# Retention and gated MLP: the first batch's V products in two steps, a new written order, single steps on other engines

## The chip, the core and the metric

The kernel runs on one NeuronCore of a Trainium2 chip. TensorE (PE, with its weight loads PEld) multiplies, VectorE (DVE), ScalarE (ACT) and GpSimd (POOL) do the elementwise work, and loads and stores go out through SP's queue. The metric is device time in microseconds, the median of three runs.

## What is computed

Inputs are q, k, v of shape (4, 8, 768, 64) in float32. A retention layer (a linear attention with a decay for each head) is followed by an MLP with a spatial gate:

```python
for t in range(S):                      # S = 768
    state = gamma * state + outer(k[t], v[t])          # per batch and head
    y[t] = scale * q[t] @ state
x = y as (4, 768, 512)
h = relu(x @ w_in);  u, v = h[..., :512], h[..., 512:]
v_n = (v - mean(v)) / sqrt(var(v) + 1e-6)
v_s = einsum('ts,bsd->btd', w_spatial, v_n) + b_spatial[None, :, None]
return (u * v_s) @ w_out
```

## The kernel before

The retention is cut into 24 groups g: four batches of six blocks of 128 positions. The MLP works on one batch at a time, in two halves of 384 positions. Most matmuls of the MLP are made of three: each operand is split into a high and a low part in a reduced float32 format (F32R), and high x high, high x low and low x high are added in PSUM. That is why every tile has a "high" cast and a "low" subtraction. The weights arrive as 64-bit words and are split on the chip as well.

The order of everything is written by hand: STEPS is one string of 1283 words. A word is a letter and a number; the letter names a step, and the last lines of the kernel call them one by one. Each engine runs its own instructions in the order in which they are written (keep, L151), so a word's place sets what it stands behind on its engine, and semaphores between engines do the rest. The letters that the text uses:

- Loads on SP: G (q and k of a group, from group 9 on the values apart by J), L (a weight slice), K (a slice of w_spatial). B loads the bias.
- Splitting weight slice i: a (absolute value, ACT), c (five DVE steps: c00 is step 0 of slice 0), H (high, ACT), R and Q (the rest and its sum, POOL or DVE by the hundreds digit: R101 is slice 1 on DVE).
- Retention: p scales the values of a group (POOL, by 2xx on ACT), q the scores, j their mask (DVE), t adds to the running total in PSUM (t1xx with the next group's scores), k copies the total to SBUF (ACT, line 371), S and x the same later on as a change that is added, y the outputs, E evicts and scales them (DVE, line 468, four of 128 columns for each group), h and l their high and low parts.
- MLP: V is one k slice (of four) of the V product of a block (V53: block 5, slice 3), r its relu, s, A, e, w, n, N the normalisation. u and z are the U product and its relu. Batch 0 multiplies with w_spatial directly (P; g, i). Batches 1 to 3 use seven products for a panel instead of eight: T sums parts (POOL, line 566), C casts one (ACT, line 582), b is its low half (DVE, line 160), M the product of nine matmuls, F and O the additions and the multiplication (DVE). M105 is product 5 of panel 0 in batch 1. f and d split the gated result, o multiplies it with w_out, Z stores.
- U is a number of matmuls on a zero tile that fill TensorE's time, m prepares the decay (m2 its rows on DVE, m0 a matmul, m1 a copy), v copies constants.

PSUM has the pools ps_r (2 banks), ps_m (3) and ps_o (3). In SBUF the split parts of products and weights live in four buffers of tag "ca" (L193): whoever allocates a fifth waits until one is free. Which buffer a tile gets is worked out when the kernel is built. All matmuls go through mm (L154), all low halves through residue (L160), so their rows are told apart by their tiles.

Of the kernel before, what the change touches and what calls it, by code (L numbers as in the profile page):

```python
# [9 lines left out]
F32 = mybir.dt.float32  # L10
# [6 lines left out]
ALU = mybir.AluOpType  # L17
# [78 lines left out]
def tile_retention_gmlp(  # L96
# [30 lines left out]
    mpool = ctx.enter_context(tc.tile_pool(name="mlp", bufs=2))  # L127
    ps_r = ctx.enter_context(tc.tile_pool(name="ps_r", bufs=2, space=bass.MemoryType.PSUM))
# [33 lines left out]
    def pick(n):  # L162
        return (nc.gpsimd, nc.vector, nc.scalar)[int(n)]

# [68 lines left out]
    def split_high(i):  # L233
        keep(nc.scalar.copy(doubles[i][0], halves[i][1]))
# [35 lines left out]
    def spatial_high(n, s):  # L270
        keep(nc.scalar.copy(parts_sp[n][0][:, s], wholes[n][s]))

    def spatial_low(n, s):
        high, low = parts_sp[n]
        keep(residue(nc.vector, low[:, s], wholes[n][s], high[:, s]))
# [93 lines left out]
    def total_copy(g, i, r):  # L369
        dst = states[g][:, 1] if i == 0 else states[g + 1][:, 0]  # L370
        keep(nc.scalar.copy(dst[ROWS[r]], total[0][ROWS[1 - r]]))
# [126 lines left out]
    def v_products(b, c, ks=range(KT)):  # L498
        xh, xl = xhalf[b, c // TT]
        cols = slice((c % TT) * P, (c % TT) * P + P)  # L500
        if not ks[0]:
            norm[b, c] = ps_m.tile([P, DM], F32, tag="m", name=f"v{b}_{c}")
# [421 lines left out]
```

## Time and profile before

| what | value |
|---|---|
| median of 3 runs | 370.76 us (370.67 to 370.95) |
| the profiled execution | 371.19 us |
| its span, first to last instruction | 369.2 us |
| TensorE busy | 360.7 us, 98% |
| VectorE busy | 240.2 us, 65% |
| ScalarE busy | 156.0 us, 42% |
| POOL busy | 115.0 us, 31% |

Times in the profile are counted from the first instruction. A row of the timeline gives the start, the length, the engine, the line, the operation, out<-in with the tiles' names, and in brackets how long the engine had been idle and what ended that. Rows of one kind in a row are merged (x3). A matmul is drawn longer than the distance to the next one, since matmuls are pipelined, and each one in float32 or F32R on 64 rows is recorded as two. Shares of busy time are averages over stages with different limits, so the table by stage stands beside them.

### The profile page before, as it was taken

To read this page: it belongs to the slowest core of one execution; us is meant where nothing else is said; L and a number is where in the kernel's file an instruction comes from. 1 tells how busy PE (TensorE), PEld (TensorE's weight loads), DVE (VectorE), ACT (ScalarE), POOL (GpSimd) and SP (SyncE) were. 2 spreads that over 40 slices of the span, in tenths; PEclk is the share of its full clock that TensorE was granted. 3 is DMA by queue.
4 is the path that set the end of the run, shared out by engine and by line. 5 is a ranking of instruction groups with operands and counts; after the bars stand their busy time and mean duration, and the time that the engine had idled before them with its cause. 6 is when DMAs were issued, how large, how long until landed. Compare 5 with 4: busy or idle time off the path is not lost.

```text
span 369.2 us, 10325 instructions
## 1 busy us (share of the span) xinstructions
PE 360.7 (98%) x4425; PEld 314.6 (85%) x4428; DVE 240.2 (65%) x533; ACT 156.0 (42%) x322; POOL 115.0 (31%) x121
## 2 busy tenths in 40 slices
PE   7889999999999999999999999999999999999995
PEld 3678885879888889999988889999998888999885
DVE  2999999598866677697685563278575443165631
ACT  4698784443412355632323246242133245432232
POOL 3523621461054224242325341233142321404011
PEclk9999999999999999999999999999999999999999
DMA  8965786012253530303333114113303002000022
GB/s 305 393 236 218 293 298 279 0 33 83 95 167 115 172 142 5 115 3 115 115 117 137 63 59 144 40 76 115 118 0 135 10 2 87 0 0 2 1 87 85
DMA packets 13005, 41.20 MB, mean 112 GB/s; under 512 B 1440, under 2 KB 1696, under 8 KB 12960
## 3 DMA queue, kind: packets, MB, share of 16 engines
q1 hardware_dynamic: 12816, 40.42, 30.0%
q8 instruction: 35, 0.57, 0.6%
q10 hardware_dynamic: 144, 0.13, 0.1%
q14 instruction: 10, 0.08, 0.1%
HBM read 34.25 MB, written 6.29 MB: 110 GB/s over the span
## 4 chain that ended last, share of the span: by engine, by line
PE 95%; DVE 4%; issue 1%; DVEq 0%
PE u L154 18%; PE v L154 18%; PE o L154 18%; PE y L154 10%; PE sp L154 8%; PE x L154 6%; PE z L154 5%; PE s L154 3%; PE d L154 3%; PE w L154 3%; PE wps L734 1%; DVE room L205 1%; DVE xf L468 1%; DVE room L223 0%; DVE room L210 0%
## 5 line engine op out<-in xcount | busy, mean ns | idle before, releaser
L154 PE MATMUL u<-xh,winu_w 128*128 128x384 f32 x256 | 68.3, 338 | 0.0
L154 PE MATMUL v<-winv_w,xh 128*128 128x512 f32 x192 | 60.8, 398 | 0.0
L154 PE MATMUL o<-wout_w,gh 128*128 128x512 f32 (+1 forms) x192 | 59.8, 392 | 0.0
L468 DVE SCALAR_TENSOR_TENSOR xf<-x,decay_t,qd_t 128x128 f32<-128x128 f32 x96 | 29.2, 344 | 29.6 <-PE x L154 23.9
L154 PEld LDWEIGHTS u<-xh,winu_w 128*128 128x128 f32 x256 | 46.5, 188 | 0.7
L154 PE MATMUL u<-xl,winu_w 128*128 128x384 f32 x128 | 42.9, 335 | 0.0
L154 PE MATMUL y<-sp,a 128*128 128x384 f32 x216 | 42.0, 338 | 0.0
L154 PEld LDWEIGHTS v<-winv_w,xh 128*128 128x128 f32 x192 | 35.2, 188 | 7.5
L154 PEld LDWEIGHTS o<-wout_w,gh 128*128 128x128 f32 x192 | 35.2, 188 | 7.0
L566 POOL TENSOR_TENSOR vn<-vn 128x384 f32<-128x384 f32 x24 | 24.8, 1034 | 50.3 <-DVE a L160 41.3
L582 ACT CAST a<-vn 128x384 fp32r<-128x384 f32 x42 | 21.0, 512 | 42.9 <-POOL vn L566 28.0
L154 PEld LDWEIGHTS y<-sp,a 128*128 128x128 f32 x216 | 37.8, 188 | 0.5
L154 PE MATMUL v<-winv_w,xl 128*128 128x512 f32 x96 | 37.5, 391 | 0.0
L154 PE MATMUL o<-wout_w,gl 128*128 128x512 f32 (+1 forms) x96 | 37.3, 389 | 0.0
L160 DVE TENSOR_TENSOR a<-vn,a 128x384 fp32r<-128x384 f32 x42 | 23.6, 576 | 13.0 <-ACT a L582 12.8
L532 POOL TENSOR_TENSOR rs<-rs,mhalf 128x1 f32<-128x1 f32 x24 | 15.0, 628 | 50.3 <-DVE rs L528 47.4
L643 ACT ACTIVATE ur<-u 128x384 f32<-128x384 f32 x32 | 15.2, 487 | 36.0 <-PE u L154 32.4
L345 POOL TENSOR_TENSOR vk<-vk,decay_t 128x512 f32<-128x512 f32 x17 | 18.7, 1103 | 34.3 <-DMA vk<-in_float_dram 34.3
L519 DVE BATCH_NORM_STATS2 bst<-vr 128x6 f32<-128x512 f32 x24 | 16.4, 687 | 18.3 <-ACT vr L512 18.3
L154 PE MATMUL s<-qk 64*64 64x64 f32 x768 | 28.1, 222 | 0.0
L154 PEld LDWEIGHTS s<-qk 64*64 64x64 f32 x768 | 25.3, 137 | 2.7 <-issue 2.3
L421 DVE TENSOR_TENSOR ws<-d,ws 64x256 f32<-64x256 f32 x54 | 22.8, 422 | 6.5 <-PE d L154 5.0
(120 smaller groups left out, 673.4 us busy)
## 6 DMA issues: line engine op xcount, KB each, us to landing
qk<-in_float_dram SPq DMA_DIRECT2D x24, 512.0 KB, 4.6
vk<-in_float_dram SPq DMA_DIRECT2D x20, 512.0 KB, 4.6
raw<-in_int_dram SPq DMA_DIRECT2D x12, 512.0 KB, 6.1
out_dram<-ot SPq DMA_DIRECT2D x23, 256.0 KB, 2.1
wst<-in_float_dram SPq DMA_DIRECT2D x4, 576.0 KB, 7.5
third<-in_float_dram SPq DMA_DIRECT2D x3, 512.0 KB, 10.6
values<-in_float_dram SPq DMA_DIRECT2D x1, 552.0 KB, 4.4
bsp_t<-in_float_dram SPq DMA_DIRECT2D x1, 384.0 KB, 7.3
```

The costliest lines, as they stand in the source:

```text
L154: keep(nc.tensor.matmul(out, lhs, rhs, start=start, stop=stop, skip_group_check=shared))
L160: return eng.tensor_tensor(out, whole, high.bitcast(F32), ALU.subtract)
L205: keep(nc.vector.tensor_scalar(a, a, TOP_MAX, TOP_MIN, ALU.min, ALU.max))
L345: keep(engine.tensor_tensor(values[g], values[g], vd, ALU.mult))
L421: keep(nc.vector.tensor_tensor(dst[ROWS[r]], u, states[g][ROWS[r], i], ALU.add))
L468: nc.vector.scalar_tensor_tensor(xf[:, hp], t[hp % 2][:, hp // 2].rearrange("p i c -> p (i c)"), qg_t[:, c, hp : hp + 1], qd_t[:, hp], ALU ...
L519: keep(nc.vector.bn_stats(st, norm[b, c][0]))
L532: keep(nc.gpsimd.tensor_tensor(rs, rs, mhalf, ALU.pow))
L566: nc.gpsimd.tensor_tensor(*{7: (a11, a11, a21, ALU.subtract), 5: (a21, a21, a22, ALU.add), 6: (a21, a22, a11, ALU.subtract), 3: (a21, a12, ...
L582: keep(nc.scalar.copy(t[:, 0], part_whole(b, p, m)))
L643: keep(nc.scalar.activation(u, pu[:, :HALF], AF.Relu))
L734: keep(nc.tensor.matmul(wps, wz[:, :P], wz, start=True, stop=True))
```

## The change

The V steps of the first batch are cut in two: V10xx multiplies with the high part of the weight slice (two matmuls), V20xx with the low part (one). A block's group c = 0 evicts 256 columns at once, without the factor of the group. Steps that ran on one engine can be sent to another by a digit of the word: casts (H, h, k, X, C, f) and relus (r, z) to DVE, lows (b, Y) to POOL, sums (T) and the decay rows by choice. And all 1299 words of STEPS are written anew.

Counted over the whole string, these steps run on another engine: of C, 21 of 42 go from ACT to DVE; of f, 18 of 32; of h, 9 of 24; of z, 8 of 32; of r, 7 of 24; of X, 6 of 21; of k, 4 of 22; of H, one. Of b, 20 of 42 go from DVE to POOL, of Y 14 of 21, and the d on POOL are 19 instead of 11. Of T, 12 of 24 go from POOL to DVE, and the p are 8 on POOL, 6 on DVE and 10 on ACT instead of 19, 0 and 5. The first words, and the places that the prediction speaks of:

```diff
-    "G0 v p0 U10 q0 j0 L0 L2 a0 m2 t00 m0 k000 k001 t01 y00 U301 y01 c00 c01 c02 c03 a2 c20 c21 "
-    "c22 G1 k011 k010 H0 m1 E00 L1 U201 U101 U501 q1 p1 t10 k100 k101 a1 t11 U401 U701 G2 k111 "
...
-    "r1 p206 j6 S6 Q5 l4 V40 V41 V42 s1 A1 e0 w0 E50 E52 E51 e1 A2 E53 h5 c42 H4 V43 l105 n0 V50 "
-    "V51 V52 V53 e2 w2 c43 R104 n2 c44 Q104 N0 N2 r3 u0 r4 u1 w1 n1 s3 A3 e3 s4 A4 e4 w3 n3 N1 p7 "
...
+    "U10 U301 U201 G0 v L0 p100 U101 m102 q0 j0 t00 k1000 m0 a0 c00 c01 k001 y00 y01 L2 a2 c20 "
+    "c02 t01 c21 G1 q1 c22 j1 L1 m1 E00 E02 H0 G2 k011 G3 L3 p1 k010 c03 G4 U501 U401 U701 c23 "
...
+    "E52 s2 w0 A1 e1 V2041 V1042 n0 h5 R5 a6 j6 l105 a7 c70 A2 B w1 n1 V2042 e2 w2 V1043 V2043 "
+    "V1050 V2050 V1033 V1051 V2051 c43 c44 V1052 N0 N1 Q5 r4 V2052 s4 A4 e4 w4 G7 n2 N2 V1053 "
...
+    "T1105 C1105 p13 x1210 z11 y120 y121 E120 E122 b1105 T1106 C106 Y160 b1107 S13 b1106 x1301 "
+    "x1311 F101 T103 C103 C1102 x1300 b102 u16 z116 M105 F105 G16 M106 C1112 C104 b1103 M103 F106 "
...
+    "E142 G17 E143 h114 T1116 C116 C1117 S15 j16 O104 x1501 M111 d12 o12 F111 x1500 b116 x1510 "
+    "T113 C1113 b1113 x1511 M115 F115 M116 M113 F112 F116 F113 O113 p116 b1117 f111 M117 F117 "
...
+    "C315 M306 b1303 M303 C1304 b1304 F306 Z212 F303 O303 f130 M307 F307 O307 C1302 b302 u37 d30 "
...
+    def copied(out, src, on_vector):
+        return (nc.vector.tensor_copy if on_vector else nc.scalar.copy)(out, src)
...
+        if c == 0:
+            for n in (s // 2 for s in steps if s % 2 == 0):
+                both = t[n].rearrange("p h i c -> p h (i c)")
+                keep(nc.vector.tensor_tensor(xf[:, n::2], both, qd_t[:, n::2], ALU.mult))
+            return
...
+        high, low = winv_h[:, k], winv_l[:, k]
+        three = ((xh, high), (xh, low), (xl, high))
+        for x, w in (three, three[::2], three[1:2])[part]:
+            n = begun[b, c] = begun.get((b, c), 0) + 1
+            mm(norm[b, c], x[:, k, cols], w, start=n == 1, stop=n == 3 * KT)
...
-    def part_high(b, p, m):
+    def part_high(b, p, m, on_vector):
         t = pieces[p, m] = pair_room(F32R, f"a{b}_{p}_{m}")
-        keep(nc.scalar.copy(t[:, 0], part_whole(b, p, m)))
-
-    def part_low(b, p, m):
+        keep(copied(t[:, 0], part_whole(b, p, m), on_vector))
+
+    def part_low(b, p, m, engine):
         t = pieces[p, m]
-        keep(residue(nc.vector, t[:, 1], part_whole(b, p, m), t[:, 0]))
+        keep(residue(engine, t[:, 1], part_whole(b, p, m), t[:, 0]))
...
+        "k": lambda n: total_copy(n // 100 % 10, n // 10 % 10, n % 10, n // 1000),
...
+        "V": lambda n: v_products(*divmod(n % 1000 // 10, NC), n % 10, n // 1000),
...
+        "T": lambda n: part_sum(n // 100 % 10, n // 10 % 10, n % 10, pick(n // 1000)),
+        "C": lambda n: part_high(n // 100 % 10, n // 10 % 10, n % 10, n // 1000),
+        "b": lambda n: part_low(n // 100 % 10, n // 10 % 10, n % 10, pick(1 - n // 1000)),
```

## Rows read from the trace of the kernel before

**Rows 1.** The page: busy time by engine, and the chain that ended last.

```profile
PE 360.7 (98%) x4425; PEld 314.6 (85%) x4428; DVE 240.2 (65%) x533; ACT 156.0 (42%) x322; POOL 115.0 (31%) x121
...
PE 95%; DVE 4%; issue 1%; DVEq 0%
```

**Rows 2.** Busy time by stage: stretch, length, each engine, granted clock, DMA share.

```profile
0.00:10.00 10.00, 7.58 (x68) 3.62 (x70) 2.85 (x6) 3.83 (x7) 2.81 (x15) 1.00 0.83 315
10.00:28.00 18.00, 15.74 (x527) 12.58 (x526) 17.67 (x38) 15.43 (x46) 7.53 (x5) 1.00 0.81 310
28.00:60.00 32.00, 32.00 (x388) 25.16 (x385) 30.52 (x73) 24.50 (x55) 13.08 (x14) 1.00 0.78 291
60.00:360.00 300.00, 299.97 (x3426) 268.63 (x3425) 188.15 (x417) 110.28 (x212) 90.63 (x88) 1.00 0.21 75
360.00:369.20 9.20, 5.41 (x33) 4.58 (x31) 0.98 (x2) 1.96 (x4) 0.91 (x1) 0.96 0.24 86
```

**Rows 3.** TensorE's waits, whole span: total us, times, longest.

```profile
PE spread L154 <- DVE sown L821: 1.2, 1, 1.2
PE x L154 <- DVE third L391: 1.0, 1, 1.0
```

**Rows 4.** Timeline of the start: fills, first scores, first scaling, first mask.

```profile
1.25 4.45 PE L734 MATMUL wps<-wz 128*128 128x512 bf16 x10 [1.25 <-DVE wz L794]
5.62 1.43 PE L154 MATMUL s<-qk 64*64 64x64 f32 x26
...
5.72 1.04 POOL L345 TENSOR_TENSOR values<-values 128x512 f32<-128x512 f32 x1 [3.09 <-DMA values<-in_float_dram]
...
7.36 0.69 DVE L391 TENSOR_TENSOR ws<-s,mask_t 128x512 f32<-128x512 f32 x1 [6.17 <-PE s L154]
```

**Rows 5.** Timeline: S6 to the next V, step l105 and what follows, V50, first U.

```profile
41.45 0.23 PE L154 MATMUL s<-qk 64*64 64x64 f32 x2
...
42.49 0.50 PE L154 MATMUL v<-winv_w,xh 128*128 128x512 f32 x1
...
43.60 0.69 DVE L160 TENSOR_TENSOR xl<-xf,xh 128x512 fp32r<-128x512 f32 x1
44.21 0.21 DVE L537 TENSOR_SCALAR nb<-mv,rs 128x1 f32<-128x1 f32 x1
...
45.34 0.39 PE L154 MATMUL v<-winv_w,xh 128*128 128x512 f32 x1
...
48.06 0.33 PE L154 MATMUL u<-xh,winu_w 128*128 128x384 f32 x1
```

**Rows 6.** Groups by line and shape: busy us, mean ns, idle before and its enders.

```profile
L371 ACT COPY ws<-total 64x256 f32<-64x256 f32 x14 | 5.1, 366 | 2.8 <-PE total L154 2.7
L421 DVE TENSOR_TENSOR ws<-d,ws 64x256 f32<-64x256 f32 x54 | 22.8, 422 | 6.5 <-PE d L154 5.0
L160 DVE TENSOR_TENSOR a<-vn,a 128x384 fp32r<-128x384 f32 x42 | 23.6, 576 | 13.0 <-ACT a L582 12.8
L611 DVE TENSOR_TENSOR t<-y,bsp_t 128x384 f32<-128x384 f32 x18 | 10.0, 556 | 6.2 <-PE y L154 5.8
L566 POOL TENSOR_TENSOR vn<-vn 128x384 f32<-128x384 f32 x24 | 24.8, 1034 | 50.3 <-DVE a L160 41.3 <-ACT vn L544 8.8
L582 ACT CAST a<-vn 128x384 fp32r<-128x384 f32 x42 | 21.0, 512 | 42.9 <-POOL vn L566 28.0 <-PE y L154 7.2 <-PE z L154 6.0
```

**Rows 7.** Timeline: one DVE operation beside a POOL instruction, and alone.

```profile
16.15 1.58 POOL L242 TENSOR_TENSOR winv_w<-df,room 128x512 fp32r<-128x512 f32 x1 [2.14 <-DVE room L231]
16.53 1.49 DVE L205 TENSOR_SCALAR room<-room 128x512 f32<-128x512 f32 x1
...
20.54 0.42 DVE L205 TENSOR_SCALAR room<-room 128x512 f32<-128x512 f32 x1
```

**Rows 8.** The products of batch 1: pieces of the chain, and a cast.

```profile
158.06 1.58 PE y L154 x9
...
159.67 0.51 ACT L582 CAST a<-vn 128x384 fp32r<-128x384 f32 x1 [0.23 <-PE y L154]
```

More of the change, by code (lines that the diff above doesn't have):

```diff
@@ L127, in tile_retention_gmlp @@
     mpool = ctx.enter_context(tc.tile_pool(name="mlp", bufs=2))
+    spool = ctx.enter_context(tc.tile_pool(name="small", bufs=3))
     ps_r = ctx.enter_context(tc.tile_pool(name="ps_r", bufs=2, space=bass.MemoryType.PSUM))
@@ L163, in pick, with positive @@
         return (nc.gpsimd, nc.vector, nc.scalar)[int(n)]
+    def copied(out, src, on_vector):
+        return (nc.vector.tensor_copy if on_vector else nc.scalar.copy)(out, src)
+    def positive(out, src, on_vector):
+        if on_vector:
+            return nc.vector.tensor_scalar(out, src, 0.0, None, ALU.max)
+        return nc.scalar.activation(out, src, AF.Relu)
     doubles = [
@@ L231, in split_low, with split_high @@
         keep(nc.vector.scalar_tensor_tensor(a, low, 2.0**-52, a, ALU.mult, ALU.mult))
-    def split_high(i):
-        keep(nc.scalar.copy(doubles[i][0], halves[i][1]))
+    def split_high(i, on_vector):
+        keep(copied(doubles[i][0], halves[i][1], on_vector))
     def split_rest(i, engine):
@@ L268, in spatial_sum, with spatial_high, spatial_low @@
         parts_sp[n] = [slot(SPLIT[n][i], F32R, f"sp{n}_{i}") for i in range(2)]
-    def spatial_high(n, s):
-        keep(nc.scalar.copy(parts_sp[n][0][:, s], wholes[n][s]))
-    def spatial_low(n, s):
+    def spatial_high(n, s, on_vector):
+        keep(copied(parts_sp[n][0][:, s], wholes[n][s], on_vector))
+    def spatial_low(n, s, engine):
         high, low = parts_sp[n]
-        keep(residue(nc.vector, low[:, s], wholes[n][s], high[:, s]))
+        keep(residue(engine, low[:, s], wholes[n][s], high[:, s]))
     queries = {}
@@ L367, in total_sum, with total_copy @@
                 )
-    def total_copy(g, i, r):
+    def total_copy(g, i, r, on_vector):
         dst = states[g][:, 1] if i == 0 else states[g + 1][:, 0]
-        keep(nc.scalar.copy(dst[ROWS[r]], total[0][ROWS[1 - r]]))
+        keep(copied(dst[ROWS[r]], total[0][ROWS[1 - r]], on_vector))
     def score(g, i, hp, r):
@@ L476, in out_evict, with out_half @@
             )
-    def out_half(g, low, engine=None):
+    def out_half(g, low, engine=None, on_vector=False):
         b, c = divmod(g, NC)
@@ L484, in out_half @@
         else:
-            keep(nc.scalar.copy(xh[:, :, cols], outs[g]))
+            keep(copied(xh[:, :, cols], outs[g], on_vector))
     def split3(pairs, ps, start=True, stop=True):
@@ L496, in tile_retention_gmlp, with v_products, v_relu @@
     norm = {}
-    def v_products(b, c, ks=range(KT)):
+    begun = {}
+    def v_products(b, c, k, part=0):
         xh, xl = xhalf[b, c // TT]
         cols = slice((c % TT) * P, (c % TT) * P + P)
-        if not ks[0]:
+        if (b, c) not in begun:
             norm[b, c] = ps_m.tile([P, DM], F32, tag="m", name=f"v{b}_{c}")
-        split3(
-            [((xh[:, k, cols], xl[:, k, cols]), (winv_h[:, k], winv_l[:, k])) for k in ks],
-            norm[b, c],
-            start=not ks[0],
-            stop=ks[-1] == KT - 1,
-        )
-    def v_relu(b, c):
+        high, low = winv_h[:, k], winv_l[:, k]
[3 more added lines that the diff above has]
+            mm(norm[b, c], x[:, k, cols], w, start=n == 1, stop=n == 3 * KT)
+    def v_relu(b, c, on_vector):
         v = mpool.tile([P, DM], F32, tag="v", bufs=3, name=f"vr{b}_{c}")
-        keep(nc.scalar.activation(v, norm[b, c], AF.Relu))
+        keep(positive(v, norm[b, c], on_vector))
         norm[b, c] = [v]
     def v_stats(b, c):
-        st = mpool.tile([P, 6], F32, tag="bst", bufs=2, name=f"bst{b}_{c}")
-        mv = mpool.tile([P, 2], F32, tag="mv", bufs=3, name=f"mv{b}_{c}")
-        rs = mpool.tile([P, 1], F32, tag="rs", bufs=3, name=f"rs{b}_{c}")
+        st = spool.tile([P, 6], F32, tag="bst", bufs=2, name=f"bst{b}_{c}")
+        mv = spool.tile([P, 2], F32, tag="mv", name=f"mv{b}_{c}")
+        rs = spool.tile([P, 1], F32, tag="rs", name=f"rs{b}_{c}")
         keep(nc.vector.bn_stats(st, norm[b, c][0]))
@@ L535, in v_bias @@
         v, mv, rs, _ = norm[b, c]
-        nb = mpool.tile([P, 1], F32, tag="nb", bufs=3, name=f"nb{b}_{c}")
+        nb = spool.tile([P, 1], F32, tag="nb", name=f"nb{b}_{c}")
         keep(nc.vector.tensor_scalar(nb, mv[:, 0:1], rs, -1.0, ALU.mult, ALU.mult))
@@ L561, in corners, with part_sum @@
         return [vn[b][:, s, d] for d in cols for s in rows]
-    def part_sum(b, p, m):
+    def part_sum(b, p, m, engine):
         a11, a12, a21, a22 = corners(b, p)
         keep(
-            nc.gpsimd.tensor_tensor(
+            engine.tensor_tensor(
                 *{
@@ L638, in mlp_u, with u_relu @@
         us[b, half, j] = pu
-    def u_relu(b, j, half):
+    def u_relu(b, j, half, on_vector):
         pu = us[b, half, j]
         u = mpool.tile([P, HALF], F32, tag="u", name=f"ur{b}_{j}_{half}", bufs=6)
-        keep(nc.scalar.activation(u, pu[:, :HALF], AF.Relu))
+        keep(positive(u, pu[:, :HALF], on_vector))
         us[b, half, j] = u
@@ L667, in gate_product @@
     def gate_product(b, j, half):
-        pp, u = gate[b, half, j], us[b, half, j]
+        pp = gate[b, half, j]
         t = mpool.tile([P, HALF], F32, tag="t", name=f"t{b}_{j}_{half}", bufs=3)
@@ L671, in gate_product, with gate_high @@
         keep(nc.vector.tensor_tensor(t, pp[:, :HALF], bsp_t[:, cols], ALU.add))
-        gate[b, half, j] = t, u
+        gate[b, half, j] = t
     def gate_times(b, j, half):
-        t, u = gate[b, half, j]
+        t, u = gate[b, half, j], us[b, half, j]
         keep(nc.vector.tensor_tensor(t, t, u, ALU.mult))
         gate[b, half, j] = t
-    def gate_high(b, j, half):
+    def gate_high(b, j, half, on_vector):
         t = gate[b, half, j]
         gh = mpool.tile([P, HALF], F32R, tag="gh", name=f"gh{b}_{j}_{half}")
-        keep(nc.scalar.copy(gh, t))
+        keep(copied(gh, t, on_vector))
         gate[b, half, j] = (t, gh)
@@ L738, in tile_retention_gmlp @@
     steps = {
-        "m": lambda n: (decay_spread, decay_copy, decay_rows)[n](),
+        "m": lambda n: (
+            decay_rows(pick(n // 100)) if n % 100 == 2 else (decay_spread, decay_copy)[n]()
+        ),
         "v": lambda n: consts_copy(),
@@ L747, in tile_retention_gmlp @@
         "c": lambda n: splits[n % 10](n // 10),
-        "H": split_high,
+        "H": lambda n: split_high(n % 100, n // 100),
         "R": lambda n: split_rest(n % 100, pick(n // 100)),
@@ L754, in tile_retention_gmlp @@
         "t": lambda n: total_sum(n // 10 % 10, n % 10, n >= 100),
-        "k": lambda n: total_copy(n // 100, n // 10 % 10, n % 10),
+        "k": lambda n: total_copy(n // 100 % 10, n // 10 % 10, n % 10, n // 1000),
         "U": lambda n: warm(n % 100),
@@ L760, in tile_retention_gmlp @@
         "E": lambda n: out_evict(n // 10, [n % 10]),
-        "h": lambda n: out_half(n, False),
+        "h": lambda n: out_half(n % 100, False, None, n // 100),
         "l": lambda n: out_half(n % 100, True, pick(n // 100)),
-        "V": lambda n: v_products(*divmod(n // 10, NC), [n % 10]),
-        "r": lambda n: v_relu(*divmod(n, NC)),
+        "V": lambda n: v_products(*divmod(n % 1000 // 10, NC), n % 10, n // 1000),
+        "r": lambda n: v_relu(*divmod(n % 100, NC), n // 100),
         "s": lambda n: v_stats(*divmod(n, NC)),
@@ L773, in tile_retention_gmlp @@
         "W": spatial_sum,
-        "X": lambda n: spatial_high(n // 10, n % 10),
-        "Y": lambda n: spatial_low(n // 10, n % 10),
+        "X": lambda n: spatial_high(n // 10 % 10, n % 10, n // 100),
+        "Y": lambda n: spatial_low(n // 10 % 10, n % 10, pick(1 - n // 100)),
         "u": lambda n: mlp_u(n // 10, *units[n % 10]),
-        "z": lambda n: u_relu(n // 10, *units[n % 10]),
+        "z": lambda n: u_relu(n // 10 % 10, *units[n % 10], n // 100),
         "P": lambda n: spatial_products(0, *units[n]),
@@ L780, in tile_retention_gmlp @@
         "i": lambda n: gate_times(0, *units[n]),
-        "T": lambda n: part_sum(n // 100, n // 10 % 10, n % 10),
-        "C": lambda n: part_high(n // 100, n // 10 % 10, n % 10),
-        "b": lambda n: part_low(n // 100, n // 10 % 10, n % 10),
+        "T": lambda n: part_sum(n // 100 % 10, n // 10 % 10, n % 10, pick(n // 1000)),
+        "C": lambda n: part_high(n // 100 % 10, n // 10 % 10, n % 10, n // 1000),
+        "b": lambda n: part_low(n // 100 % 10, n // 10 % 10, n % 10, pick(1 - n // 1000)),
         "M": lambda n: product(n // 100, n // 10 % 10, n % 10),
@@ L786, in tile_retention_gmlp @@
         "O": lambda n: product_times(n // 100, n // 10 % 10, n % 10),
-        "f": lambda n: gate_high(n // 10, *units[n % 10]),
+        "f": lambda n: gate_high(n // 10 % 10, *units[n % 10], n // 100),
         "d": lambda n: gate_low(n // 10 % 10, *units[n % 10], pick(n // 100)),
@@ L814, in tile_retention_gmlp, with decay_rows @@
         )
-    def decay_rows():
+    def decay_rows(engine):
         n = NP * P // C
@@ L820, in decay_rows @@
         rows = rows_t.rearrange("p (c n) -> p c n", n=n)
-        keep(nc.vector.tensor_tensor(rows, eye, own, ALU.mult))
+        keep(engine.tensor_tensor(rows, eye, own, ALU.mult))
     def decay_spread():
```

111 rows, old and new, of the table STEPS are left out of this document.

## Prediction, made before the change was run

> **What bounds the kernel now.** I read the page's busy line and chain first, then a table of engine time by stage, then what TensorE waited for. The page says TensorE: it is busy for 98% of the span, and the chain that ended last is 95% TensorE [rows 1]. The table by stage says where the other 2% are. From 60 to 360 us TensorE is busy for 299.97 of 300 us; from 28 to 60 us for 32.00 of 32; before 28 us it lacks 2.4 + 2.3 us; the end lacks 3.8 us, which is the last copy and store [rows 2]. "Busy" hides gaps shorter than a matmul's drawn length, so I also compared the starts: twelve matmuls of the last V block run from 45.34 to 48.06 us, 0.227 us each, back to back, and nine matmuls of a product take 1.58 us, a wait-free pace [rows 5, 8]. So after 28 us there is nothing to win short of fewer matmuls. The waits before that are few; the longest are 1.2 us for the decay rows and 1.0 for a mask [rows 3].
>
> Who makes TensorE wait there is read from the same table: from 10 to 28 us VectorE is busy for 17.67 of 18 us and ScalarE for 15.43; from 28 to 60 us VectorE for 30.52 of 32 [rows 2]. In the first 45 us VectorE is as much a bound as TensorE, and after 60 us it is not (188 of 300 us).
>
> **The change, part by part.** The written order of TensorE's work holds the same matmuls: each of the 24 V steps of the first batch keeps its three, as two and one. The 18 fill matmuls stay 18. So TensorE's own work changes by nothing, and the forecast is a sum of waits: in the start, where VectorE decides, and later, where new waits can come.
>
> *The start.* I follow VectorE to one step, l105, the low half of block 5, without which TensorE can't begin that block's V products. Before, l105 starts at 43.60, the next instruction follows at 44.21, and V50 starts at 45.34, about 1.05 us after l105 ends: TensorE comes last [rows 5]. VectorE ran the 74 instructions ahead of l105, and l105 itself, from 7.36 (first mask) to 44.21, 36.9 us [rows 4, 5]. Adding them up at their spacing in a full queue gives 32.4; 4.5 us are collisions and waits. The new order puts 79 ahead instead: four copies of the running total (0.42 each by the nearest VectorE row of that size, 0.37 on ScalarE, [rows 6]: 1.7), the first scaling (0.6), one more sum Q102 (0.6), the cast h103 (0.4), against two evictions of 256 columns for four of 128 (-0.2) and a few small ones (-0.1): 3.0 us more, 35.4 in all.
>
> Two of these, the scaling and the decay rows (1.2 us), now run while VectorE stood idle, from about 5.72, when the first values are there [rows 4]. But three fill matmuls move ahead of the first scores. Ten took 4.45 us, 0.43 each, and the first scores came at 5.62 [rows 4]; three more end at 6.8 if they keep that pace. The granted clock is full in that stretch [rows 2], yet 0.43 is what 512 columns take at 1.2 GHz, while V's 512 columns take 0.227 later, near 2.4 GHz [rows 5]: the engine was at the lower level. Part of the delay comes back, because the scores then run at the faster pace. I take the first mask at 7.95 (bounds 7.4, no delay, and 8.7, all of 1.3). From there 34.2 us of queue remain ahead of the end of l105. If nothing collided or waited, it would end at 42.2; with all of the old 4.5 us at 46.7. I take 2.4: eight long POOL instructions instead of eleven stand ahead of it, and POOL causes most of the 4.5. So 44.6, against 44.2 before.
>
> What is worth the same differs, though. At V50 TensorE had done S6 (about 1.04 us, from 41.45 to 42.49) and 2.7 us of V were left [rows 5]; in the new order S6 comes later and ten V steps, 3.4 us, are left. The moment of equal progress is 45.34 - 1.04 - 0.7 = 43.6. With V1050 at 44.7 the start **loses 1.1 us**. Bounds: a gain of 1.4 (l105 at 42.2) and a loss of 3.2 (46.7). ScalarE points the same way: the scalings p202, p203 and p204 stay on it, each behind copies that wait for TensorE, and t20, t130 and t140 wait for them.
>
> *Casts on VectorE behind buffers.* Twenty-one casts of product parts (C) move from ScalarE to VectorE. The parts live in four buffers of tag ca, so a cast can have to wait until a product ends. The trace shows it on ScalarE: its casts idled 7.2 and 6.0 us for products y and z, for example the one at 159.67, as the product of 158.06 ends [rows 6, 8]. There nothing urgent is queued behind it. On VectorE the additions F are, and a product that accumulates into the same bank waits for its F. Three places in the new order have this form. (1) C1102 stands ahead of x1300, b102, z116 and F105; if its buffer is that of M105, VectorE needs 0.35 + 0.42 + 0.58 + 0.56 + 0.56 = 2.5 us after M105 [rows 6], while only M106 (1.58) covers it before M103: 0.9 us. (2) C1117 waits for M111, then j16, O104, x1501, F111, x1500, b116, POOL's T113 (1.03), C1113 and POOL's b1113 (1.04) must run before M113: about 6.0 us, against 5.2 of cover by o12, M115 and M116: 0.8. (3) C1304 stands ahead of F306 and may wait for M303; M307 is next: 0.35 + 0.56 = 0.9. A cast of 384 columns is not in the trace on VectorE; 0.35 is scaled from its 0.42 for 512, and 0.55, a two-input one, is the other bound [rows 6, 7]. Which cast gets which buffer is fixed when the kernel is built, and I can't read it from the order: each of the three is worth nothing if another cast gets the freed buffer. Together 0 to 2.6; I take **1.3 us lost**.
>
> *Lows on POOL, sums on VectorE.* 34 low halves (20 b, 14 Y) go to POOL, where an instruction of that size takes 1.03 instead of 0.58, and 12 sums T come back [rows 6]. I followed the queues around all products: apart from the three places the lows have over 0.4 us to spare, so I cost them at nothing; the cover is the product before. If it is gone, each costs about 0.5. Here a row speaks against the change: VectorE's clamp takes 0.42 alone, and 1.49 when POOL's sum started 0.38 us ahead of it [rows 7]. The Trainium skill (SBUF — State Buffer, SBUF: two separate sides) says that the two engines share a port pair that one of them holds for its whole instruction while the other blocks, and names VectorE's copies in the two-port mode and its operations on two SBUF inputs; the trace agrees. By that rule alone every meeting of a POOL low with a VectorE cast would cost up to 1.1 us; the sum leaves this to the third rival, priced by the rows.
>
> *Nothing else.* The gate's late read of u, the new pool of small tiles and the first block's evictions without a factor change no queue that ends last. Loads move on SP's queue (L3 now behind a wait for the first qk buffer, L5 and K earlier); their users come over 4 us later. The end (o37, copies, stores) is as before.
>
> **The sum.** Against the profiled execution, 371.19 us with a span of 369.2: 371.19 + 1.1 + 1.3 = 373.6. The median of the runs is 370.76, 0.43 less, so I forecast 373.2 us.
>
> **The rivals.** (a) *The start wins.* VectorE idles until 7.36 now and loses 4.5 us to collisions and waits (one of them is in [rows 7]); if both go, l105 ends at 42.2, 1.4 us are won and no cast waits: 371.19 - 1.4 - 0.43 = 369.4. For it: POOL has less ahead of l105. Against it: 3.0 us more on an engine that is already full. It decides once l105 ends before 43.5. Chance 0.28. (b) *The start draws and the buffers fall kindly*, or the change doesn't do what it says since VectorE sets the start either way: 370.8. Chance 0.14. (c) *Collisions in the product chains.* If six of the 20 products whose low half is now on POOL each wait 0.6 us for it behind a VectorE instruction, 3.6 us come on top of the start's 1.1: 375.5. For it: 1.49 against 0.42. Against it: after 60 us both engines have idle time. Chance 0.10. The forecast itself, 371.3 to 374.9: 0.48.
>
> **How the numbers follow.** 0.2% is 0.74 us, about what a measurement of this kernel can tell from no change. Faster: (a), 0.28. Same: (b), 0.14. Slower: the forecast and (c), 0.58. The range goes from 369.4, the end of (a), to 376.5: the start's loss of 3.2 and the casts' 2.6 on the median, 376.6, rounded.
>
> **What would show it.** First mask near 8.0 us. l105's end, the last V product of batch 0 near 48 us, and TensorE's progress there 1 us behind. TensorE waits of 0.5 to 1 us for VectorE F or POOL low halves between 145 and 190 us and near 320 us, where there are none now. The forecast is wrong if l105 ends before 43.5, or if TensorE shows no waits after 60 us and the time is below 370.0.

## The result and the profile after

The changed kernel takes 376.18 us (375.92 to 376.43), against 370.78 for the kernel before: 1.0145 of it (95% interval 1.0127 to 1.0163), 5.4 us slower. I had forecast slower, by 2.4 us. The profiled execution has a span of 374.6 us, 5.4 over the 369.2 of before.

The page first: busy time by engine, and the chain that ended last.

```profile
PE 362.2 (97%) x4428; PEld 315.0 (84%) x4428; DVE 261.8 (70%) x579; ACT 129.5 (35%) x288; POOL 129.2 (34%) x136
...
PE 87%; DVE 5%; DMA 3%; ACT 2%; issue 1%; SPq 1%; POOL 0%; DVEq 0%
```

TensorE's share of the chain fell from 95% to 87% [rows 1]: there are now places where something else comes last. The table by stage (columns as in [rows 2]; the last two rows are shorter stretches) says where.

```profile
0.00:10.00 10.00, 8.56 (x131) 4.62 (x133) 4.11 (x9) 3.97 (x7) 1.77 (x14) 1.00 0.82 315
10.00:28.00 18.00, 16.00 (x434) 13.10 (x432) 14.89 (x35) 13.37 (x38) 5.12 (x4) 0.91 0.91 344
28.00:60.00 32.00, 31.56 (x414) 25.86 (x414) 30.67 (x78) 23.89 (x57) 13.23 (x14) 1.00 0.77 292
60.00:360.00 300.00, 295.23 (x3396) 261.94 (x3395) 207.16 (x453) 85.25 (x182) 106.02 (x102) 1.00 0.20 70
...
15.00:18.00 3.00, 3.00 (x80) 3.00 (x80) 1.31 (x3) 0.56 (x2) 1.39 (x1) 0.50 0.92 367
145.00:200.00 55.00, 52.49 (x735) 49.01 (x734) 43.20 (x93) 12.18 (x28) 24.08 (x24) 1.00 0.25 88
```

From 60 to 360 us TensorE now lacks 4.8 us, where it lacked 0.03 [rows 2]. Up to 10 us it does more than before; from 10 to 28 us it is busy for as long, but at a lower granted clock. TensorE's waits by what ended them (total us, times, longest):

```profile
PE z L159 <- DVE t L630: 2.5, 2, 1.4
PE s L159 <- DMA qk<-in_float_dram: 1.5, 2, 1.3
...
PE y L159 <- DVE t L630: 1.2, 1, 1.2
PE x L159 <- issue: 1.1, 1, 1.1
```

Three waits for an addition F (line 630), 3.7 us together; one for a load in the start; and one, "issue", for nothing that the profile shows.

A lag worked out from the matmul starts puts them in time. I price each matmul still to come at the mean spacing of its kind in the kernel before after 70 us, look up when that kernel had the same work left, and take the difference. It is good to some 0.3 us. (Rows: kernels of the experiments below; columns: us in the kernel's own time.)

```
                      45   145   165   192   260   270   330   340
changed              0.9   0.7   2.4   3.3   2.7   4.1   4.1   5.5
e2_casts_later       1.3   1.8   1.9   1.2   0.8   2.6   2.7   2.5
e5_start_load       -0.1   0.0   1.5   2.2   2.0   4.3   4.3   5.7
e7_lows_vector       1.5   2.3   4.8   7.1  11.4  11.3  13.8  14.5
e10_load_only        1.1   1.1   1.0   0.5   0.1   0.8   0.8   0.6
```

So the changed kernel loses 0.9 us in the start, 1.7 between 145 and 165 us, 0.9 up to 192, 1.4 at 265 and 1.4 at 332. It wins back 0.2 before 145 us and 0.6 between 192 and 260, for which I have no row.

**The three waits for F.** VectorE, TensorE and GpSimd at the first place, C1102:

```profile
158.74 1.73 PE L159 MATMUL y<-sp,a 128*128 128x384 f32 x9
158.94 0.55 DVE L171 CAST a<-vn 128x384 fp32r<-128x384 f32 x1 [1.61 <-PE z L159]
159.27 1.01 POOL L165 TENSOR_TENSOR a<-vn,a 128x384 fp32r<-128x384 f32 x1 [0.63 <-ACT a L171]
159.52 0.43 DVE L434 TENSOR_TENSOR ws<-d,ws 64x256 f32<-64x256 f32 x1
159.87 0.82 DVE L165 TENSOR_TENSOR a<-vn,a 128x384 fp32r<-128x384 f32 x1
160.71 0.56 DVE L175 TENSOR_SCALAR ur<-u 128x384 f32<-128x384 f32 x1
161.18 0.55 DVE L630 TENSOR_TENSOR t<-z,bsp_t 128x384 f32<-128x384 f32 x1
161.88 0.41 PE L159 MATMUL z<-sp,a 128*128 128x384 f32 x1 [1.41 <-DVE t L630]
```

The cast idles 1.61 us until the product z (M105) has let go of its buffer. Behind it stand x1300, the low b102 (0.82), z116 and only then F105; M103 starts at 161.88, when F105 has ended. M106 (158.74, nine matmuls of 0.17) would have let it start at 160.3: 1.6 us lost. At the third place, C1304, the same happens with F306; at the second the chain from b116 over T113 and C1113 ends with F115 at 188.5, and M113 starts:

```profile
182.29 0.55 DVE L171 CAST a<-vn 128x384 fp32r<-128x384 f32 x1 [0.67 <-PE y L159]
...
185.91 1.01 POOL L585 TENSOR_TENSOR vn<-vn 128x384 f32<-128x384 f32 x1 [8.53 <-DVE a L165]
186.96 0.55 DVE L171 CAST a<-vn 128x384 fp32r<-128x384 f32 x1 [0.78 <-POOL vn L585]
187.59 1.97 POOL L165 TENSOR_TENSOR a<-vn,a 128x384 fp32r<-128x384 f32 x2 [0.67 <-DVE a L171]
188.59 1.66 PE L159 MATMUL z<-sp,a 128*128 128x384 f32 x8 [1.10 <-DVE t L630]
...
332.92 0.55 DVE L171 CAST a<-vn 128x384 fp32r<-128x384 f32 x1 [3.62 <-PE z L159]
333.39 0.55 DVE L630 TENSOR_TENSOR t<-y,bsp_t 128x384 f32<-128x384 f32 x1
334.00 1.33 PE L159 MATMUL y<-sp,a 128*128 128x384 f32 x6 [1.18 <-DVE t L630]
```

Start to start, TensorE loses 1.58, 1.26 and 1.34 us at the three places: 4.2.

**The load in the start.** The first scores come at 5.83 and the first mask at 7.03, ahead of [rows 4]; but q2 then stands ahead of its load, which is issued when it was before (4.14 us), and the granted clock falls to 0.50 from 15 to 18 us (above). That fall is not what makes the kernel slower: it is in the profiled execution, whose mean granted clock is 0.994, and the other three, at 0.998 to 1.000, take 375.92 to 376.42 us.

```profile
13.31 0.33 PE L159 MATMUL x<-qk,ws 64*64 64x64 f32 x6
14.90 0.37 PE L159 MATMUL s<-qk 64*64 64x64 f32 x2 [1.26 <-DMA qk<-in_float_dram]
...
43.78 0.68 DVE L165 TENSOR_TENSOR xl<-xf,xh 128x512 fp32r<-128x512 f32 x1
```

The last row is l105: 43.78, where it was 43.60 [rows 5]. The early scores come from the fills, whose starts stand 0.43 us apart up to 4.7 us and 0.22 after it. The record of the granted clock begins only at that moment (4.66 us), so the 1.00 in the row of the first ten microseconds, here and in [rows 2], does not say at which level the first fills ran. In the profiles of the experiments this record begins anywhere from 4.1 to 7.2 us, and where it begins at 6.9 or later all 13 fills stand 0.43 apart.

**The stop at 265.** Six matmuls of a group of eight, a stop, and the last two:

```profile
264.80 0.30 PE L159 MATMUL x<-qk,ws 64*64 64x64 f32 x6
266.18 0.32 PE L159 MATMUL x<-qk,ws 64*64 64x64 f32 x2 [1.08 <-issue]
```

### The profile page after: what moved, and what is told of

Read it like the earlier page. It is cut to its first block, busy times and chain, and to the rows that moved or that the text cites. A ratio compares the mean times of both kernels' runs of the same rounds, so it can differ in the third digit from the quotient of the medians.

```text
span 374.6 us, 10326 instructions
## 1 busy us (share of the span) xinstructions
PE 362.2 (97%) x4428; PEld 315.0 (84%) x4428; DVE 261.8 (70%) x579; ACT 129.5 (35%) x288; POOL 129.2 (34%) x136
## 4 chain that ended last, share of the span: by engine, by line
PE 87%; DVE 5%; DMA 3%; ACT 2%; issue 1%; SPq 1%; POOL 0%; DVEq 0%
PE u L159 18%; PE o L159 17%; PE v L159 16%; PE y L159 9%; PE sp L159 8%; PE x L159 5%; PE z L159 5%; PE s L159 4%; DMA qk<-in_float_dram 3%; PE w L159 3%; PE d L159 1%; SPq L162 1%; DVE a L171 1%; DVE t L630 1%; DVE xf L486 1%
## 5 line engine op out<-in xcount | busy, mean ns | idle before, releaser
L159 PE MATMUL u<-xh,winu_w 128*128 128x384 f32 x256 | 70.0, 340 | 0.0
L165 POOL TENSOR_TENSOR a<-vn,a 128x384 fp32r<-128x384 f32 x20 | 22.1, 1110 | 50.2 <-DVE a L171 27.4
L486 DVE SCALAR_TENSOR_TENSOR xf<-x,decay_t,qd_t 128x128 f32<-128x128 f32 x80 | 24.3, 345 | 11.5 <-PE x L159 8.0
L159 PE MATMUL s<-qk 64*64 64x64 f32 x768 | 29.7, 224 | 1.5 <-DMA qk<-in_float_dram 1.5
L563 ACT ACTIVATE vn<-vr,nb,rs 128x512 f32<-128x512 f32 x24 | 19.2, 815 | 28.5 <-DVE nb L556 25.0
L165 POOL TENSOR_TENSOR xl<-xf,xh 128x512 fp32r<-128x512 f32 x13 | 17.9, 1379 | 30.3 <-ACT xh L171 14.8
L551 POOL TENSOR_TENSOR rs<-rs,mhalf 128x1 f32<-128x1 f32 x24 | 13.9, 587 | 41.1 <-DVE rs L547 40.5
L165 POOL TENSOR_TENSOR gl<-ur,gh 128x384 fp32r<-128x384 f32 x16 | 16.8, 1052 | 28.2 <-DVE gh L171 13.4
L171 ACT CAST a<-vn 128x384 fp32r<-128x384 f32 x21 | 10.8, 516 | 42.4 <-PE z L159 15.0
L159 PEld LDWEIGHTS u<-xl,winu_w 128*128 128x128 f32 x128 | 24.0, 188 | 0.7
```

The costliest lines, as they stand in the source:

```text
L159: keep(nc.tensor.matmul(out, lhs, rhs, start=start, stop=stop, skip_group_check=shared))
L165: return eng.tensor_tensor(out, whole, high.bitcast(F32), ALU.subtract)
L171: return (nc.vector.tensor_copy if on_vector else nc.scalar.copy)(out, src)
L486: nc.vector.scalar_tensor_tensor(xf[:, hp], t[hp % 2][:, hp // 2].rearrange("p i c -> p (i c)"), qg_t[:, c, hp : hp + 1], qd_t[:, hp], ALU ...
L551: keep(nc.gpsimd.tensor_tensor(rs, rs, mhalf, ALU.pow))
L563: keep(nc.scalar.activation(vn[b][:, c], v, AF.Identity, bias=nb, scale=rs))
```

## The experiments

Moves in the written order are given as the words that change place. The times are medians, with the lowest and highest in brackets; each ratio is against the kernel before on the same chip.

**Casts to ScalarE.**

```diff
-C1102 ... C1117 ... C1304
+C102 ... C117 ... C304
```

> The changed kernel with three of its 21 moved casts put back on ScalarE at the same written places: C1102, C1117 and C1304. Theory (a cast that waits for its buffer on VectorE holds the addition F that TensorE's next product needs): the TensorE waits of 1.58 us at 160, 1.26 at 187 and 1.34 at 332 go, 376.2 - 4.2 = 372.0 us; the 1.3 us stop at 265 stays. Rival (VectorE and GpSimd are simply too full in the product chains, the casts only happen to stand there): the waits come back at other products, 375 us or more.

Measured 375.10 us (374.88 to 375.57), 1.0114 [1.0098, 1.0129]: neither theory's number. The third wait is gone, the second is 0.33, the first is as long as it was. The trace of the first place:

```profile
158.79 0.93 ACT L171 CAST a<-vn 128x384 fp32r<-128x384 f32 x2 [2.21 <-POOL vn L585]
158.86 1.73 PE L159 MATMUL y<-sp,a 128*128 128x384 f32 x9
159.39 1.02 POOL L165 TENSOR_TENSOR a<-vn,a 128x384 fp32r<-128x384 f32 x1 [0.62 <-ACT a L171]
159.76 1.06 DVE L165 TENSOR_TENSOR a<-vn,a 128x384 fp32r<-128x384 f32 x1 [1.85 <-ACT a L171]
161.31 0.55 DVE L630 TENSOR_TENSOR t<-z,bsp_t 128x384 f32<-128x384 f32 x1
162.00 0.41 PE L159 MATMUL z<-sp,a 128*128 128x384 f32 x1 [1.41 <-DVE t L630]
```

The cast now waits on ScalarE, but its low b102 is one of those left on VectorE, ahead of F105, and waits for the cast: 1.85 us idle, then 1.06 beside GpSimd's low. What counts is not which engine waits for the buffer, but that anything that depends on it stands ahead of F on VectorE.

**Casts behind the additions.**

```diff
-C1102 x1300 b102 u16 z116 M105 F105
+x1300 u16 z116 M105 F105 C1102 b102
-C1117 ... M115 F115
+M115 F115 C1117
-C1304 b1304 F306
+F306 C1304 b1304
```

> The changed kernel with the same three casts left on VectorE, but written behind the addition that they held: C1102 and its low b102 behind F105, C1117 behind F115, C1304 and its low b1304 behind F306. If the place in VectorE's queue is the cause, all three waits go, 372.0 us as with the casts on ScalarE. If it is the engine (0.55 us for a cast there, beside GpSimd's lows), 375 us or more.

Measured 373.48 us (372.53 to 374.05), 1.0066 [1.0045, 1.0086]. All three waits for F are gone, with the casts still on VectorE, and the lag doesn't rise from 145 to 260 us. TensorE's longest waits, one for a zero tile in the start left out:

```profile
PE x L159 <- issue: 1.7, 2, 1.3
...
PE x L159 <- DVE xf L482: 0.8, 1, 0.8
```

And at the first place, the timeline: F105 (160.01) runs as soon as M105 has ended, and M103 (161.38) follows M106 without a gap.

```profile
158.26 1.72 PE L159 MATMUL z<-sp,a 128*128 128x384 f32 x9
159.82 1.72 PE L159 MATMUL y<-sp,a 128*128 128x384 f32 x9
160.01 0.56 DVE L630 TENSOR_TENSOR t<-z,bsp_t 128x384 f32<-128x384 f32 x1 [0.57 <-PE z L159]
161.38 1.03 PE L159 MATMUL z<-sp,a 128*128 128x384 f32 x5
```

The place in the queue is shown as the cause. The median gains 2.7 us rather than 4.2. In its profile the start was 1.1 us later (lag at 145: 1.8 against 0.7): its 13 fills took 5.51 us, and 4.65 in the changed kernel. That would be most of the difference, if the other executions, of which there is no trace, started as late; this is not shown. Over all profiles with the three fills ahead the 13 take from 4.37 to 5.73 us, and the first scores begin from 5.5 to 6.9 us.

**The output products apart.**

```diff
-S21 ... y200 y201 M215
+S21 ... M215 y200 y201
```

> The changed kernel with the output products y200 and y201 moved behind the product M215, so that they no longer follow the step S21 directly. Theory (TensorE stopped for 1.3 us at 265 because the unbroken run of short 64-row matmuls of S21, y200 and y201 uses up its instructions faster than they come): the stop goes, 376.2 - 1.3 = 374.9 us. Rival (it belongs to a spot in the instruction stream or to the output and load transfers begun at that moment): a stop of the same size stays close by, 376.2 us.

Measured 377.02 us (375.43 to 377.50), 1.0149 [1.0120, 1.0179]: no gain. The stop inside y201 is gone, as the theory said, but M211 follows y201 now and waits 0.8 us for an output eviction (1.0 start to start):

```profile
PE y L159 <- DVE xf L486: 0.8, 1, 0.8
```

**V in one step again.**

```diff
-V1000 ... V2000
+V00
```

(and so for all 24, each at the place of its second part)

> The changed kernel with the first batch's V products in one step again, each standing where its second part (the low half of the weights) stood. TensorE is full from 28 us on, so what the split brings can only be idle time before that: V1000 filled 0.45 us at 18.5, and one or two more first parts stand ahead of their second. Theory: the split is worth about 0.5 to 1 us, 376.7 to 377.2 us. Rival (VectorE up to l105 sets the start whatever TensorE does before): 376.2 us.

Measured 377.53 us (376.76 to 378.38), 1.0178 [1.0156, 1.0200], 0.3% over the changed kernel's ratio, as the theory has it, though the two intervals overlap. The lag at 32 us is 1.9, against 0.8, and stays at 2.0. But this profile's fills took 5.73 us, 1.1 more than the changed kernel's, and a kernel with V split and fills as slow (the one with o22 moved, below) has a lag of 2.2 at 60 us too. So the split helps early, by some 1 us at 32, and what is left of it at the end of the start is between nothing and 1.2 us: not settled.

**The load G2 first.**

```diff
-L1 m1 E00 E02 H0 G2
+G2 L1 m1 E00 E02 H0
-a1 c10 Q0 L5 k100 k101 j2
+Q0 L5 k100 k101 a1 j2 c10
```

> The changed kernel with one change in its start: the load G2 is issued ahead of L1, and the weight clamp's two first steps a1 and c10, which use L1, stand behind k101 and j2. In the changed kernel TensorE waited 1.45 us at 13.4 us for this load and then ran at a granted clock of 0.50 from 15 to 18 us. Theory (that wait costs the start its whole loss): the wait goes and the start wins about 1 to 1.5 us, 374.7 to 375.2 us. Rival (VectorE up to l105 sets the end of the start, the wait lies beside it): TensorE idles somewhere else before 45 us and the time stays 376.2 us.

Measured 376.62 us (375.87 to 377.79), 1.0147 [1.0118, 1.0175]: the time is the rival's. Its profile isn't: the lag is about 0 from 45 to 145 us. The rows of l105 (a timeline) and of the stretch from 10 to 28 us (the table by stage):

```profile
42.98 0.68 DVE L165 TENSOR_TENSOR xl<-xf,xh 128x512 fp32r<-128x512 f32 x1
```

```profile
10.00:28.00 18.00, 14.89 (x455) 12.12 (x449) 16.22 (x37) 14.41 (x42) 5.52 (x4) 1.00 0.95 353
```

l105 starts 0.8 us earlier than in the changed kernel, with the same instructions ahead of it, and VectorE is busy for 16.22 us instead of 14.89: it followed the load, not its own length. In the same profile the 0.7 us are lost again at 262: S21 waits 0.6 us start to start, for G22's load by the next experiments. Whether all its executions did, the single profile can't say. The rival is right in part, too: TensorE now stops inside q2's scores, for 0.8 us at 14.1, and for 0.5 at 19.6, both "issue" (last section).

**Casts mended, o22 behind S21.**

```diff
-o22 l18 x2000 ... S21
+l18 x2000 ... S21 o22
```

> The changed kernel with the three casts behind their additions (372.5 to 374.1 us alone) and, for the stop at 265, the output product o22 moved behind the step S21, so that 12 long matmuls stand between the short ones of S21 and those of y200 and y201. Theory (the stop comes when short matmuls run on without a break until an instruction block has to be fetched): the stop of 1.3 to 1.5 us goes, 372.1 us. Rival (the stop moves to the next wait, as when the y steps stood behind M215): 373.5 us.

Measured 375.08 us (372.78 to 376.33), 1.0085 [1.0047, 1.0123]. The stop inside y201 is gone again, and again something takes its place: S21, 2.7 us earlier in TensorE's order, waits for its load.

```profile
261.75 0.33 PE L159 MATMUL s<-qk 64*64 64x64 f32 x4 [1.29 <-DMA qk<-in_float_dram]
```

Its executions fall in two groups. Two, at a mean granted clock of 1.000, take 372.8 us, near the 372.1 of the theory; three, at 0.949 (the profiled one) to 0.995, take 375.1 to 376.3. No trace shows the first two.

**Lows back to VectorE, sums back to GpSimd** (on the kernel with the casts mended).

```diff
-b1101 ... b1317 (20 words)   T1105 ... T1316 (12 words)
+b101 ... b317               T105 ... T316
```

> The changed kernel with the three casts behind their additions, and the engines of two other kinds of step undone: the 20 low halves b back from GpSimd to VectorE, the sums T back from VectorE to GpSimd. Theory of the prediction (these moves cost nothing in the product chains): 373.5 us, the same within 0.5. Rival (GpSimd's lows beside VectorE's casts cost TensorE time after 100 us): faster, 372.5 us or less. Third (VectorE, now fuller, makes TensorE wait): 374.5 us or more.

Measured 384.35 us (381.25 to 385.52), 1.0337 [1.0287, 1.0388]: 11 us slower than with the casts behind alone, the third theory, and far beyond it. TensorE waits for lows and casts of the product parts:

```profile
PE y L159 <- DVE a L165: 2.0, 1, 2.0
...
PE z L159 <- DVE a L165: 1.2, 1, 1.2
...
PE y L159 <- ACT a L171: 0.8, 1, 0.8
```

In this written order the two moves together aren't merely free: the order rests on them. Lows and sums were moved back at once, so no run says how much of the 11 us is due to either. The rival, by which the lows' collisions with VectorE cost time, predicted a gain and is not borne out; the one collision seen, 0.25 us in the low ahead of F105, is part of the first wait.

**Three mends together** (G2 first, casts behind, o22 behind S21).

> The changed kernel with all three mends: G2 ahead of L1, the three casts behind their additions, o22 behind S21. If the three are independent and each brings what its theory says: 376.2 - 4.2 - 1.3 - 1.2 = 369.5 us, below the kernel before (370.8). If the start is set by VectorE whatever the load does: 370.7 us. If the stop only moves: 372 us.

Measured 372.83 us (372.32 to 374.92), 1.0049 [1.0024, 1.0074]. The lag is -0.1 at 145 us and -0.7 at 220; then S21 stands 1.7 us for G22, which SyncE issues at 253.5, behind J21 and a store, and the kernel ends 1.1 us behind.

**G22 ahead of J21 as well.**

```diff
-J21 Z112 G22
+G22 J21 Z112
```

> As the kernel with three mends (G2 ahead of L1, three casts behind their additions, o22 behind S21), with a fourth: the load G22 is issued ahead of J21. With three mends TensorE stood 1.7 us at 257 ahead of S21, while G22's load had been issued only at 253.5, behind J21 and a store on SyncE's queue. Theory: that was the load, the wait goes, and the time is 372.8 - 1.7 = 371.1 us, 0.999 of the kernel before. Rival (VectorE or a buffer holds S21): 372.8 us, 1.004.

Measured 374.98 us (374.01 to 376.54), 1.0105 [1.0082, 1.0127]: slower, against both. S21's scores now have their load, but its updates d wait 2.0 us for the scaled values, which come with J21; and the granted clock falls to 0.97 over 260 to 320 us, in the output products behind that wait. Moving S21 forward was wrong: it has two loads to wait for.

**The same with o22 ahead of S21 again.**

> G2 ahead of L1, the three casts behind their additions, G22 ahead of J21, but o22 back ahead of S21, so that S21, y200 and y201 follow each other again. Theory (the stop inside y201 comes from the unbroken run of short matmuls, whatever is loaded when): the stop of 1.3 to 1.5 us is there again at about 260, 1.3 to 1.5 us slower than the kernel with all four. Rival (the stop belongs to the late load): no stop, the same time as with all four.

Measured 371.68 us (371.26 to 373.30), 1.0026 [1.0013, 1.0039]: the best of these kernels so far, 0.8 us behind the kernel before. The stop is there, but of 0.6 us start to start: between the two theories.

```profile
262.27 0.30 PE L159 MATMUL x<-qk,ws 64*64 64x64 f32 x4
262.93 0.33 PE L159 MATMUL x<-qk,ws 64*64 64x64 f32 x2 [0.36 <-issue]
```

What this tells of the stop is in the last section. This kernel differs from the one with only the casts behind in the two loads put ahead, G2 (with a1 and c10 behind it) and G22: 1.0026 [1.0013, 1.0039] against 1.0066 [1.0045, 1.0086]. So the loads are worth about 0.4%, 1.5 us, in time, both together.

**G1 ahead of L2** (on the kernel with all four mends).

> The kernel with all four mends and one more: the load G1 is issued ahead of L2, so the second block's scores and values come ahead of the second piece of weights. In the start TensorE still stands about 1 us at 11.3 for values that arrive at 11.2. If loads set the start: up to 1 us less than with all four, 370.1 us, 0.996 of the kernel before. If VectorE's queue up to l105 sets it, or the weights come too late now: the same or 0.5 to 1 us more.

Measured 375.81 us (375.18 to 377.99), 1.0134 [1.0111, 1.0156]. The lag at 45 us is 2.0, against 0.2 with all four mends; but the fills of this profile took 5.73 us, and against experiment 10's, whose fills took as long (lag 1.1), only 0.9 is left for the loads. The weights come too late, as the second theory said: ScalarE stands 1.3 us for a piece of them at 11.0, and VectorE 1.6 behind it. From 10 to 28 us the DMA engines are busy for 0.89 to 0.96 in all kernels with the new order, and for 0.81 before [rows 2], so a load put ahead can delay another. The order of the first loads isn't simply "scores first".

**The three fills behind the first sums** (on e10's kernel).

```diff
-U10 U301 U201 G0 v L0 p100 U101 m102 q0 j0 t00 k1000 m0
+U10 G0 v L0 p100 m102 q0 j0 t00 U301 k1000 m0 U201 U101
```

> The best kernel so far (G2 ahead of L1, the three casts behind their additions, G22 ahead of J21; 371.7 us, 1.0026 of the kernel before) with the three single fills that the change had put ahead of the first scores moved behind the first sums: U301 behind t00, U201 and U101 behind the spread m0, where TensorE waits anyway. Theory of the prediction (each fill ahead of the scores can cost up to 0.43 us; 13 of them took from 4.4 to 5.7 us in the runs): the first scores come at 5.6 us in every run, the time goes down by 0.3 to 0.8 us to 370.9 to 371.4, level with or just below the kernel before. Rival (VectorE up to l105 doesn't start earlier, or the fills delay the first outputs instead): 371.7 us as before.

Measured 371.63 us (370.99 to 372.81), 1.0021 [1.0008, 1.0035], the same as without. The first scores come at 5.62, as the theory said, and the time doesn't follow. In its profile TensorE stops for 1.9 us (start to start) inside q2's scores at 14; no load ends that stop but "issue", 1.45 us after a packet of 16 KB of the instruction queue (13.42 to 14.51), as with the stop at 265 (last section):

```profile
15.96 0.46 PE L159 MATMUL s<-qk 64*64 64x64 f32 x5 [1.66 <-issue]
```

The profiled execution took 372.62 us, 1 us over the median, so the others may have stopped for less. None of the kernels beats the one before.

## Why the prediction was wrong in size and right in direction

*What bounds the kernel.* Right: nothing was to be won after 28 us, and what was added there shows in full.

*The start, 1.1 us lost.* The sum came out near (0.7 to 0.9 in the profile, l105 at 43.78, its end at 44.5 against my 44.6) by luck, for other reasons. The first mask was at 7.03, not 7.95, since the 13 fills ran faster here than I had them; in other kernels' profiles with the same fills it was at 7.0 to 8.2. VectorE wasn't the bound that the sum took it for: from 10 to 28 us it is busy for 14.89 us, and 17.67 before [rows 2]. What came last was G2's load. I had checked the loads that move, and found 4 us to spare; I hadn't checked the one that stays while its user q2 moves ahead of it. That is the step that failed here. Its price is about 0.8 us in profiles: where the fills are as fast, the lag at 145 us is 0.0 to 0.3 with G2 first (experiments 5, 8 and 9) and 0.7 to 1.4 without (the changed kernel, 1 and 3). In time it shows only together with G22, 1.5 us for both (experiment 10).

*Casts behind buffers, 1.3 us lost of 0 to 2.6.* The mechanism, the three places, the F held at each and the product that waits for it were right: M103, M113 and M307 wait, and no other product does. The size was off, 4.2 against 1.3, in two steps. First, I halved the sum because I couldn't see which cast gets which buffer; all three got the one named. Without the halving it is 2.6. Second, the cast itself. I scaled 0.35 us from a contiguous operation and called 0.55 a bound. The groups by shape:

```profile
L171 DVE CAST a<-vn 128x384 fp32r<-128x384 f32 x21 | 11.5, 549 | 14.2 <-PE z L159 7.8 <-POOL vn L585 4.1 <-ACT vn L563 1.4
L171 DVE CAST gh<-t 128x384 fp32r<-128x384 f32 x6 | 2.2, 359 | 1.0 <-PE o L159 0.7
L165 DVE TENSOR_TENSOR a<-vn,a 128x384 fp32r<-128x384 f32 x22 | 12.4, 571 | 5.0 <-ACT a L171 4.8
```

A cast of 384 contiguous columns does take 0.36; the casts of the product parts take 0.55, as much as an operation with two inputs. Their source is three pieces of 128 columns out of vn. The Trainium skill (VectorE: DVE Perf Modes, Mode 2×_2P — use both read ports for one tensor) says that a copy gets its double rate by splitting its outermost dimension between two ports, if that is even, or equal in source and destination; with three pieces on one side and a whole run on the other it would fall back to the single rate. The two rows agree. A third does too: the cast xh, whose source is four pieces of 128, takes 0.46 for 512 columns, the pace of the contiguous one.

```profile
L171 DVE CAST xh<-xf 128x512 fp32r<-128x512 f32 x9 | 4.1, 464 | 0.1
```

No run here changed the pieces. Four such casts stand in the three chains: 0.2 us each is 0.8 of the 1.6 between 2.6 and 4.2. The low beside GpSimd's is another 0.24 (0.82 for 0.58); the rest, some 0.5 us over the three, lies at the hand-overs between engines and was not measured one by one. The Trainium skill's lock of the port pair (SBUF — State Buffer, SBUF: two separate sides), by which a VectorE operation on two SBUF inputs waits for GpSimd's whole instruction, fits these lows: 0.82 and 1.06 us beside GpSimd, 0.57 on average, and both end 0.41 us after GpSimd's low has ended.

*Lows on POOL at nothing.* Right as a cost, and short: putting both back costs 11 us.

*Nothing else.* Wrong. The stop at 265 (1.3 us) is neither a load nor another engine: TensorE's next instructions had not come (last section). The sum had no term for it, so it stood at nothing. I had also cost the loads' moves at nothing, by their users' distance and not by what stands ahead of them on SyncE's queue: G22 goes behind J21, which waits for a buffer, and behind a store. That cost 0.2 us in the changed kernel, and 0.6 to 1.7 where S21 came earlier (experiments 5, 6 and 8).

*The range and the rivals.* 376.18 is inside 369.4 to 376.5, at its upper end. Rival (a) is out: the start lost in the profile. Rival (c), at 375.5, comes nearest in time, but not by its mechanism: in the changed kernel collisions set no wait by themselves. In short, the step that failed is the casts' term, halved to 1.3 us where 4.2 were measured, and after it "nothing else", which hid a stop of 1.3.

## What to carry to other kernels

Before an operation is put on another engine's queue, list what it may wait for, and what stands behind it there: a wait that cost nothing on an idle engine is paid in full where the accumulating product's addition is next. Moving only the waiting step isn't enough; all that depends on it has to go behind as well. And when a step is moved forward, look at the loads that don't move: its own, and what is queued ahead of it.

## What the runs showed of the hardware

The stop inside y201 ends with an instruction block. In the changed kernel a packet of 16 KB on the queue that the page calls "instruction" is the only one in its stretch, 263.7 to 264.0 us:

```profile
q8 instruction: 1, 0.02, 20.0%
```

It starts at 263.82 and takes 0.96 us, so it ends at 264.78, and TensorE goes on at 266.18. In all eight kernels whose trace has the stop (the changed one and the experiments 1, 2, 4, 5, 7, 10 and 12) TensorE goes on 1.33 to 1.54 us after the end of such a packet, while the stop itself is 0.6 to 1.6 us long; it is always the same two matmuls, and it is gone where long matmuls stand between S21 and y201. In every profile this queue moves 35 packets of 16 KB, and TensorE's instructions, 8943 to 8957 in the traces, make 35 blocks of 256. The stop lies at the 7360th of them, and the other stops that end with "issue", in the start (0.3 to 1.9 us, the one of experiment 12 among them), at the 448th, 704th, 960th or 1472nd, each within two: always a multiple of 256 apart, and always 1.3 to 1.7 us after such a packet. So TensorE had run through a block of instructions before the next one was there. The Trainium skill (Runtime: NRT & Kernel Launch, Instruction fetch mechanics) says that instructions are fetched in blocks of 16 KiB and that the cost of crossing into the next is mostly hidden; here it was not, for 1.3 us.

The run of short matmuls alone isn't enough: the kernel before runs S21, y200 and y201 unbroken as well, from 260.2 to 262.3 us, and doesn't stop, for its packet had ended at 259.50. What the kernels with the stop share is that they were through a block before its successor could come. Their packet starts 0.9 to 2.1 us after TensorE enters the block before it, takes 0.9 to 1.3, and the 1.33 to 1.54 come on top: 3.5 us or more in all. The changed kernel went through that block in 2.4 us; the kernel before, with long matmuls in it, in 3.9. What sets the moment of the packet stays open: in experiment 10 it came 0.1 us ahead of S21 (stop 0.6), in the others 0.8 to 1.3 us behind S21's start. No run moved a packet alone, so this account rests on the traces' counts and times.

After the wait of 1.26 us at 13.6 us the granted clock was 0.50 from 14.9 to 18.3 us (the lower of its two levels, 1.2 GHz); after waits about as long at 160 and 187 us it stayed at 1.00. In experiment 12 it fell the same way after the stop at 14, from 16.0 to 19.4 us.
